# Key, value and weight loads of a one-token attention block: issued by GpSimd in place of SyncE

## Chip, core and metric

The kernel runs on one core of one Trainium2 chip. The metric is the device time of one execution in microseconds (us). Three runs of the kernel before are given; what is compared is their median. The trace comes from one further execution under the profiler.

## What is computed

One decoding step of a transformer block for a single token (width 640): layer norm, attention with 32 heads over a cache of 8192 keys and values of width 192, output projection, residual, layer norm, a gated ReLU network of width 1536, residual. All is float32.

```python
def _A_ref(x, k_cache, v_cache, wq, wo):
    q = (x @ wq).reshape(B, Sq, H, Dh).transpose(0, 2, 1, 3)
    scores = einsum("bhqd,bhkd->bhqk", q, k_cache) * (Dh ** -0.5)
    o = einsum("bhqk,bhkd->bhqd", softmax(scores), v_cache)
    return o.transpose(0, 2, 1, 3).reshape(B, Sq, H * Dh) @ wo
def _B_ref(x, W_gate, W_up, W_down):
    gate = x @ W_gate; up = x @ W_up
    return ((gate * (gate > 0)) * up) @ W_down
h  = x + _A_ref(_layernorm(x), k_cache, v_cache, wq, wo)
h2 = h + _B_ref(_layernorm(h), W_gate, W_up, W_down)
```

Keys and values are 2 x 32 x 8192 x 192 floats, 403 MB; the weights add the rest of some 446 MB. Each number of them is read once and used once, against a single query.

## The kernel before

The host packs everything into a few long arrays of 128 rows, in the order in which it is used: `row_p` (the first head's keys, query weights, the token), then ten turns of five pieces `row_1` to `row_5`, then the last head and the weights of the network (`row_t1` to `row_t3`, `row_up`, `row_gate`, `row_down`). A piece is at most 128 rows of 16320 floats, 65280 bytes a row. On the chip there are three buffers of that size, `slot_x`, `slot_y` and `slot_z` (X, Y, Z in the code), and each load fills one of them.

A turn (`turn`, ten of them) works through three heads: `pe_unit` on TensorE multiplies a head's keys by its query (L180) and, for the head before, its values by the softmax weights (L187); VectorE makes the next query and adds the output projection (`dve_unit`); ScalarE takes the exponentials. The loops of the engines run beside each other, tied by semaphores.

All 61 loads are issued by SyncE, in `sync_program`, through `load`. Three loads go out at once (`row_p` into Y, the first `row_1` into X, the first `row_2` into Z). From then on SyncE waits, before it refills a buffer, for a semaphore `free[..]` that says the buffer has been read to its end, and for `land[..]`, which the earlier load into it raised by 16; it takes the 16 off again in the same wait. The order is Y (`row_3`), X (`row_4`), Y (`row_5`), X (`row_1`), Z (`row_2`). After the last turn come ten loads of the tail, each with a semaphore of its own in `tl`, which TensorE waits for and takes down. At the end SyncE waits for `fout`, stores half of the result, and waits until both halves are stored (`out_s`, `out_a`; ScalarE stores the other half).

GpSimd has little to do: `pool_program` makes four constants (`ones`, `ident`, `pat`) and raises `cst_pe` and `cst_ve`, for which TensorE and VectorE wait before they start.

Of the kernel before, what the change touches and what calls it, by code (L numbers as in the profile page):

```python
# [8 lines left out]
ET = mybir.EngineType  # L9

P, D, H, S, DH, F = 128, 640, 32, 8192, 192, 1536
# [7 lines left out]
NTURN = (H - 2) // 3  # L19
SCALE = DH ** -0.5  # L20
EPS = 1e-5
DG, FG = D // 4, F // 4

W_P = 14272
# [61 lines left out]
def build(nc, arrays):  # L86
# [31 lines left out]
    o4 = sb("o4", [P, DG])  # L118
# [14 lines left out]
    def wait(eng, s, n, sub=0, **kw):  # L133
        w = eng.wait_ge(s, n)  # L134
        if sub:
            w.then_inc(s, -sub)
        return w
# [37 lines left out]
    te = nc.tensor  # L175
# [37 lines left out]
    def pe_unit(kblk, vblk, rows, freed=None, freed_at=None, q_next=True):  # L213
        def landed(n):
            if n in rows:
                s, sub = rows[n]
                wait(te, s, 16, sub)

        wait(te, a2p, 1, 1)
        landed("k0")  # L220
        pe_k(kblk, 0)
        wait(te, a2p, 1, 1)
        pe_o()
        wait(te, a2p, 1, 1)
        pe_l()
        landed("k1")
        pe_k(kblk, 1)
        landed("v0")
        at = None if freed is None else (freed_at, freed)
        pe_v(vblk, 0, 8, inc_at=at)  # L230
        landed("v8")
        pe_v(vblk, 8, 24, inc_at=at)
        if q_next:
            wait(te, d2p, 2, 2)
            if freed is not None and freed_at < 24 and freed is not fin:
                te.sem_inc(freed, 1)
            pe_q()
        else:
            wait(te, d2p, 1, 1)
        pe_t()  # L240
        landed("v24")
        pe_v(vblk, 24, 32, last=p2a)

    def tensor_program():
        wait(te, cst_pe, 1, 1)
        wait(te, pre, 1, 1)
        op(te.matmul(pl[:, 0:1], ones, vec["s1"], start=True, stop=True), inc=p2d)
        wait(te, pre, 1, 1)
        op(te.matmul(pl[:, 0:1], ones, vec["s2"], start=True, stop=True), inc=p2d)
        wait(te, d2p, 1, 1)  # L250
        pe_q()
        wait(te, a2p, 1, 1)
        wait(te, land[5], 16)
        pe_k(kp, 0)
        pe_k(kp, 1)
        wait(te, d2p, 2, 2)
        pe_q()
        pe_t()
        with te.Fori(0, NTURN):
            pe_unit(ka, va, {"k0": (land[1], 0), "v8": (land[2], 0)}, free[1], 7)  # L260
            pe_unit(kb, vb, {"k1": (land[3], 0), "v24": (land[4], 0)}, free[3], 23)
            pe_unit(kc, vcc, {"v0": (land[5], 0)})
        pe_unit(kt, vt, {"k0": (tl["t1"], 16), "v8": (tl["t2a"], 16)}, fin, 7, q_next=False)
        wait(te, a2p, 1, 1)
        pe_o()
        wait(te, a2p, 1, 1)
        pe_l()
        wait(te, tl["t2b"], 16, 16)
        pe_v(vz, 0, 16)
        wait(te, d2p, 3, 3)  # L270
        for g in range(4):
            te.matmul(acc[Q(g), 0:DG], ones[Q(g), 0:32], xd[Q(g)].rearrange("p c j -> p (c j)"),
                      start=True, stop=False, tile_position=(32 * g, 32 * g))
        for g in range(4):
            te.matmul(acc[Q(g), 0:DG], ones[:, 0:32], accs[:, g * DG:(g + 1) * DG], start=False, stop=False)
        for g in range(4):
            r = slice(0, 64) if g < 2 else slice(64, P)
            te.matmul(acc[Q(g), 0:DG], ones[r, 0:32], accs[r, D + (g % 2) * DG:D + (g % 2 + 1) * DG],
                      start=False, stop=False)
        wait(te, tl["t3"], 16, 16)  # L280
        pe_v(vz, 16, 32, last=p2a)
        wait(te, a2p, 1, 1)
        pe_o()
        wait(te, d2p, 1, 1)
        for g in range(4):
            te.matmul(acc[Q(g), 0:DG], oc[:, 0:1].to_broadcast([P, 32]), woz[:, g * DG:(g + 1) * DG],
                      start=False, stop=False)
        for g in range(4):
            r = slice(0, 64) if g < 2 else slice(64, P)
            m = te.matmul(acc[Q(g), 0:DG], oc[r, 1:2].to_broadcast([64, 32]),  # L290
                          woz[r, D + (g % 2) * DG:D + (g % 2 + 1) * DG], start=False, stop=True)
        m.then_inc(p2a, 1)
        wait(te, a2p, 1, 1)
        op(te.matmul(pt[:, 0:1], ones, vec["hs1"], start=True, stop=True), inc=p2d)
        wait(te, d2p, 1, 1)
        op(te.matmul(od[:, 0:1], ones, vec["hs2"], start=True, stop=True), inc=p2d)
        wait(te, tl["up"], 16, 16)
        for j in range(DJ):
            for g in range(4):
                m = te.matmul(sc[Q(g), 0:FG], hc[:, j, :], up[:, j, g * FG:(g + 1) * FG],  # L300
                              start=(j == 0), stop=(j == DJ - 1))
        op(m, inc=p2a)
        wait(te, tl["gate"], 16, 16)
        for j in range(DJ):
            for g in range(4):
                m = te.matmul(sc[Q(g), 512:512 + FG], hc[:, j, :], gate[:, j, g * FG:(g + 1) * FG],
                              start=(j == 0), stop=(j == DJ - 1))
        op(m, inc=p2d)
        wait(te, d2p, 1, 1)
        wait(te, tl["d0"], 16, 16)  # L310
        for j in range(FJ):
            if j == 6:
                wait(te, tl["d1"], 16, 16)
            if j == 10:
                wait(te, tl["d2"], 16, 16)
            if j < FJ - 1:
                for g in range(4):
                    te.matmul(q_ps[Q(g), 0:DG], guT[:, j, :], down[:, j * D + g * DG:j * D + (g + 1) * DG],  # L318
                              start=(j == 0), stop=False)
            else:  # L320
                for half in range(2):
                    if half:
                        wait(te, tl["d3"], 16, 16)
                    for g in range(2 * half, 2 * half + 2):
                        m = te.matmul(q_ps[Q(g), 0:DG], guT[:, j, :], down[:, j * D + g * DG:j * D + (g + 1) * DG],  # L325
                                      start=False, stop=True)
        op(m, inc=p2d)
# [199 lines left out]
        po_.sem_inc(cst_pe, 1)  # L527
        po_.sem_inc(cst_ve, 1)

    sp = nc.sync  # L530

    def load(t, src, s):
        sp.dma_start(t, src).then_inc(s, 16)

    def sync_program():
        load(Y[:, 0:W_P], dram["row_p"], land[5])
        r1, r2, r3, r4, r5 = (dram[f"row_{i}"] for i in range(1, 6))
        load(X[:, 0:W_1], r1[0], land[1])
        load(Z[:, 0:W_2], r2[0], land[2])

        def turn(i):
            wait(sp, free[5], 1, 1)
            wait(sp, land[5], 16, 16)
            load(Y[:, 0:W_3], r3[i], land[3])
            wait(sp, free[1], 2, 2)
            wait(sp, land[1], 16, 16)
            load(X[:, 0:W_4], r4[i], land[4])
            wait(sp, free[3], 2, 2)
            wait(sp, land[3], 16, 16)
            load(Y[:, 0:W_5], r5[i], land[5])  # L550
            wait(sp, free[2], 1, 1)
            wait(sp, land[2], 16, 16)
            wait(sp, free[4], 1, 1)
            wait(sp, land[4], 16, 16)

        with sp.Fori(0, NTURN - 1) as i:
            turn(i)
            load(X[:, 0:W_1], r1[i + 1], land[1])
            load(Z[:, 0:W_2], r2[i + 1], land[2])
        turn(NTURN - 1)  # L560
        load(X[:, 0:W_T1], dram["row_t1"], tl["t1"])
        load(Z[:, 0:W_T2A], dram["row_t2a"], tl["t2a"])
        load(Z[:, W_T2A:W_T2A + W_T2B], dram["row_t2b"], tl["t2b"])
        wait(sp, free[5], 1, 1)
        wait(sp, land[5], 16, 16)
        load(Y[:, 0:W_T3], dram["row_t3"], tl["t3"])
        load(Y[:, W_T3:W_T3 + W_UP], dram["row_up"], tl["up"])
        wait(sp, fin, 1, 1)
        load(X[:, 0:W_UP], dram["row_gate"], tl["gate"])
        for n, (a, b) in enumerate(DOWN):  # L570
            load(X[:, W_UP + a:W_UP + b], dram["row_down"][:, a:b], tl[f"d{n}"])
        wait(sp, fout, 1)
        load(out[0, 0, 0:D // 2].rearrange("(g n) -> g n", g=2), o4[31:33, :], out_s)
        wait(sp, out_s, 16, 16)
        wait(sp, out_a, 16, 16)
        wait(sp, fout, 1, 1)

    programs = ((ET.PE, tensor_program), (ET.DVE, vector_program), (ET.Activation, scalar_program),
                (ET.Pool, pool_program), (ET.SP, sync_program))
    for e, _ in programs:  # L580
        nc.br(f"prog_{e.name}", engines=[e])
    for e, f in programs:
# [12 lines left out]
```

## Time and profile before

| | us |
|---|---|
| median of 3 runs | 1039.3 |
| lowest and highest | 1038.07, 1039.48 |
| the profiled execution, its own time | 1039.63 |
| its span, from the first to the last instruction | 1038.3 |

1.33 us of the profiled execution's time lie outside its span. A share of busy time is an average over the span, and the DMA share is a mean over the core's 16 DMA engines. The releaser of a wait is inferred from semaphores. A transfer has two times in the trace: when its issue stands in the queue of the issuing engine, and when its landing lets a waiting engine go on. The windows view credits a packet to the stretch in which it falls only roughly, so that shares a little over 1.00 occur in short stretches.

### The profile page before, as it was taken

What the parts mean: (1) busy time and instruction counts of PE and PEld (TensorE: products, weight loads), DVE (VectorE), ACT (ScalarE), POOL (GpSimd) and SP (SyncE); (2) the same over time, 40 slices, a digit from 0 to 9 for tenths busy, and PEclk for the clock granted to TensorE, in tenths of its full rate; (3) what the DMA queues carried; (4) which work ended last, traced back from release to release, by engine and by line L of the source; (5) the groups of instructions that cost most, each with busy time, mean ns of one, the idle gap of its engine ahead of it and who ended that gap; (6) DMA issues with size and microseconds to landing.
All of it is one profiled execution on the core that took longest, in us unless ns stands there. A gap on an engine that the chain in (4) does not pass through costs nothing. (4 is left out here: it accounts for less than half of the span.)

```text
span 1038.3 us, 10306 instructions
## 1 busy us (share of the span) xinstructions
PE 547.4 (53%) x4492; PEld 176.3 (17%) x4492; DVE 188.2 (18%) x478; ACT 41.2 (4%) x137; POOL 1.2 (0%) x11
## 2 busy tenths in 40 slices
PE   0746446456363563654544546536465463564676
PEld 0211112112121120111111112112111121121123
DVE  1211221112122021221121220212221121220111
ACT  1000000000000000000000000000000000000010
POOL 0000000000000000000000000000000000000000
PEclk9876867768677677776787867867877778687787
DMA  9999999999999999999999999999999999999997
GB/s 402 441 432 425 434 435 431 445 420 435 435 439 433 425 438 436 440 427 432 435 435 426 433 438 431 444 426 433 433 438 438 420 438 436 438 432 425 432 427 326
DMA packets 8800, 446.07 MB, mean 430 GB/s; under 512 B 980, under 2 KB 1112, under 8 KB 1240
## 3 DMA queue, kind: packets, MB, share of 16 engines
q1 hardware_dynamic: 8788, 445.94, 99.4%
q8 instruction: 7, 0.11, 0.0%
q14 instruction: 1, 0.01, 0.0%
q10 hardware_dynamic: 4, 0.00, 0.0%
HBM read 445.94 MB, written 0.00 MB: 429 GB/s over the span
## 5 line engine op out<-in xcount | busy, mean ns | idle before, releaser
L180 PE MATMUL sc<-slot_x,qs 128*32 128x512 f32 x1008 | 150.9, 743 | 109.6 <-DMA slot_x<-row 99.9
L187 PE MATMUL po<-slot_y,p 128*2 128x384 f32 x1152 | 117.9, 562 | 80.2 <-DMA slot_y<-row 77.4
L187 PE MATMUL po<-slot_z,p 128*2 128x384 f32 x560 | 72.5, 671 | 91.7 <-DMA slot_z<-row 88.4
L180 PE MATMUL sc<-slot_y,qs 128*32 128x512 f32 x288 | 54.1, 913 | 83.0 <-DMA slot_y<-row 82.5
L187 PE MATMUL po<-slot_x,p 128*2 128x384 f32 x336 | 43.6, 651 | 86.1 <-DMA slot_x<-row 86.1
L373 DVE COPY oc<-od 128x2 f32<-128x2 f32 x32 | 5.1, 159 | 389.5 <-PE od L206 389.5
L385 DVE STREAM_TRANSPOSE st<-sc 128x512 f32<-128x512 f32 x64 | 45.7, 714 | 164.4 <-PE sc L180 164.4
L180 PEld LDWEIGHTS sc<-slot_x,qs 128*32 128x32 f32 x1008 | 35.4, 134 | 200.8 <-DMA slot_x<-row 106.3
L187 PEld LDWEIGHTS po<-slot_y,p 128*2 128x2 f32 x1152 | 29.1, 94 | 167.7 <-DMA slot_y<-row 86.5
L391 DVE TENSOR_REDUCE m<-pt 128x1 f32<-128x128 f32 x32 | 9.3, 292 | 162.6 <-PE pt L199 162.6
L187 PEld LDWEIGHTS po<-slot_z,p 128*2 128x2 f32 x560 | 15.0, 102 | 138.3 <-DMA slot_z<-row 95.6
L474 ACT COPY qs<-q_ps 128x96 f32<-128x96 f32 x32 | 7.7, 239 | 766.9 <-ACTq L134 766.9
L367 DVE SCALAR_TENSOR_TENSOR prod<-slot_y,xn,prod 128x192 f32<-128x192 f32 x88 | 36.9, 419 | 3.1
L180 PEld LDWEIGHTS sc<-slot_y,qs 128*32 128x32 f32 x288 | 11.4, 154 | 113.8 <-DMA slot_y<-row 83.4
L180 PE MATMUL sc<-slot_z,qs 128*32 128x512 f32 x240 | 27.6, 592 | 0.0
L187 PEld LDWEIGHTS po<-slot_x,p 128*2 128x2 f32 x336 | 8.6, 94 | 109.5 <-DMA slot_x<-row 88.0
L203 PEld LDWEIGHTS od<-mrl,ob 128*128 128x128 f32 x132 | 18.1, 199 | 34.2 <-issue 34.2
L478 ACT COPY ob<-po 128x384 f32<-128x384 f32 x32 | 15.3, 479 | 181.1 <-ACTq L134 181.1
L203 PE MATMUL od<-mrl,ob 128*128 128x1 f32 x132 | 20.8, 262 | 1.6 <-PEq L134 1.6
L194 PE MATMUL q_ps<-pat,prod 128*128 128x96 f32 x64 | 15.4, 323 | 8.5 <-PEq L134 8.5
L365 DVE TENSOR_SCALAR prod<-slot_y,xn 128x192 f32<-128x192 f32 x22 | 6.9, 315 | 65.4 <-DMA slot_y<-row 65.3
L376 DVE SCALAR_TENSOR_TENSOR accs<-slot_y,oc,accs 128x640 f32<-128x640 f32 x21 | 18.5, 879 | 0.0
(95 smaller groups left out, 248.6 us busy)
## 6 DMA issues: line engine op xcount, KB each, us to landing
slot_x<-row SPq DMA_DIRECT2D x10, 8160.0 KB, 26.9
slot_z<-row SPq DMA_DIRECT2D x10, 8160.0 KB, 45.8
slot_y<-row SPq DMA_DIRECT2D x10, 8160.0 KB, 24.7
slot_x<-row SPq DMA_DIRECT2D x10, 7680.0 KB, 35.6
slot_y<-row SPq DMA_DIRECT2D x10, 7584.0 KB, 27.1
slot_x<-row_t SPq DMA_DIRECT2D x1, 7680.0 KB, 25.2
slot_y<-row_p SPq DMA_DIRECT2D x1, 7136.0 KB, 19.6
slot_z<-row_t2a SPq DMA_DIRECT2D x1, 5088.0 KB, 36.9
```

The costliest lines, as they stand in the source:

```text
L180: m = te.matmul(sc[Q(g), half * 512:half * 512 + 512], qs[:, 32 * part:32 * part + 32], blk(half, part * 4 + g), start=(part == 0), stop=( ...
L187: m = te.matmul(po[32 * g:32 * g + 2, 0:PW], p[:, 2 * i:2 * i + 2], blk(i), start=(i < 4), stop=(i >= 28))
L194: te.matmul(q_ps[:, 0:96], prod[:, 0:P], pat[:, 0, :], start=True, stop=False)
L203: te.matmul(od[:, 0:1], ob[:, k * DH:k * DH + P], mrl[:, k:k + 1], start=(k == 0), stop=(k == 1))
L365: dv(ve.tensor_scalar(prod, w3[:, 0, :], xn[:, 0:1], None, op0=ALU.mult), w=first)
L367: dv(STT(prod, w3[:, j, :], xn[:, j:j + 1], prod, op0=ALU.mult, op1=ALU.add), w="self", inc=d2p if j == DJ - 1 else None)
L373: dv(ve.tensor_copy(oc, od[:, 0:2]), w=pd())
L376: dv(STT(accs[:, 0:D], w[:, 0:D], oc[:, 0:1], accs[:, 0:D], op0=ALU.mult, op1=ALU.add), w="self", inc=inc)
L385: return dv(ve.transpose(st[:, s], sc[:, s]), w=w)
L391: dv(ve.reduce_max(vec["m1"], pt[:, 0:P], axis=AX.X, negate=True), w=pd(), inc=d2a)
L474: op(ac.copy(qs, q_ps[:, 0:96]), inc=a2p)
L478: op(ac.copy(ob, po[:, 0:PW]), inc=a2p)
```

## The change

`load` calls GpSimd's `dma_start` instead of SyncE's. The loads, their rows, their order, their buffers and what they wait for stay as they are; they now stand in `load_program` on GpSimd, with the loop. `sync_program` keeps the store of half of the result alone. Four things go with it:

- The first three loads stand ahead of `pool_program`, so the constants are made after these three issues.
- A wait that took 16 off a load's semaphore becomes `settled`: a wait for 16, then an instruction of GpSimd's, `inc_swdge_sem`, that takes the 16 off.
- TensorE's waits on the ten semaphores of the tail no longer take them down. GpSimd does so at the end: after `fout` it runs `settled` for each of the ten, then raises `fin`.
- SyncE waits for `fin` as well before it ends.

```diff
-    def load(t, src, s):
-        sp.dma_start(t, src).then_inc(s, 16)
+    def load(t, src, s, **kw):
+        po_.dma_start(t, src, single_packet=SINGLE, **kw).then_inc(s, 16)
+
+    def settled(s):
+        wait(po_, s, 16)
+        po_.inc_swdge_sem([s], [16], mode="sub")
...
         load(Z[:, 0:W_2], r2[0], land[2])
+        pool_program()
...
-            wait(sp, free[5], 1, 1)
-            wait(sp, land[5], 16, 16)
+            wait(po_, free[5], 1, 1)
+            settled(land[5])
             load(Y[:, 0:W_3], r3[i], land[3])
...
-        with sp.Fori(0, NTURN - 1) as i:
+        with po_.Fori(0, NTURN - 1) as i:
...
+        wait(po_, fout, 1)
+        for s in tl.values():
+            settled(s)
+        po_.sem_inc(fin, 1)
...
         wait(sp, out_a, 16, 16)
+        wait(sp, fin, 1, 1)
```

`SINGLE` is False. TensorE's waits on `tl`, such as `wait(te, tl["up"], 16, 16)`, become `wait(te, tl["up"], 16)`.

GpSimd's queue at the start of the program, in the kernel before: five instructions of the preamble, a branch, and the constants (`ones`, `pat`, `ident`; `cst` is the semaphore between them).

```order
L581 UNCONDITIONAL_BRANCH [waits barrier_Pool_Activation_PE_DVE_SP_gather]
L519 MEMSET ones 128x128
L520 MEMSET pat 128x288
L522 ISA
L522 AFFINE_SELECT ident<-ones 128x128 [waits cst]
L525 MEMSET pat 128x16 x4
```

The same place in the changed kernel, on to the first refill of a buffer (the lines of the code are shifted).

```order
L594 UNCONDITIONAL_BRANCH [waits barrier_Pool_Activation_PE_DVE_SP_gather]
L532 DMA slot_y<-row_p 128x14272
L532 DMA slot_x<-row 128x16320
L532 DMA slot_z<-row 128x16320
L520 MEMSET ones 128x128
L521 MEMSET pat 128x288
L523 ISA
L523 AFFINE_SELECT ident<-ones 128x128 [waits cst]
L526 MEMSET pat 128x16 x4
L560 UNCONDITIONAL_BRANCH [waits cst]
L536 ISA [waits free5,land5]
```

Three DMA issues stand where `ones` was made, and the constants behind them; the instruction at L536, which takes 16 off a semaphore, is the first of the loop and holds the two waits of the first refill.

The end of SyncE's queue before: the last loads of the tail and the store of the result.

```order
L533 DMA slot_x<-row_gate 128x7680 [waits fin]
L533 DMA slot_x<-row_down 128x3840
L533 DMA slot_x<-row_down 128x2560
L533 DMA slot_x<-row_down 128x960
L533 DMA slot_x<-row_down 128x320
L533 DMA out<-o 2x160 [waits fout]
```

The end of GpSimd's queue now: the same loads, and behind them the ten instructions that wait for `fout` and take the semaphores of the tail down (seven of them are shown; three more, for `tl_d1` to `tl_d3`, follow).

```order
L532 DMA slot_x<-row_down 128x960
L532 DMA slot_x<-row_down 128x320
L536 ISA [waits tl_t1,fout]
L536 ISA [waits tl_t2a]
L536 ISA [waits tl_t2b]
L536 ISA [waits tl_t3]
L536 ISA [waits tl_up]
L536 ISA [waits tl_gate]
L536 ISA [waits tl_d0]
```

The store of half of the result stays on SyncE, alone there behind `fout`; the ten instructions run on GpSimd beside it.

## Rows read from the trace of the kernel before

**Rows 1.** The page: DMA share in 40 slices, packets, and the loads' queue.

```profile
DMA  9999999999999999999999999999999999999997
...
DMA packets 8800, 446.07 MB, mean 430 GB/s; under 512 B 980, under 2 KB 1112, under 8 KB 1240
...
q1 hardware_dynamic: 8788, 445.94, 99.4%
```

**Rows 2.** Windows: stretch, its length, five engines' busy us, PEclk, DMA share, GB/s.

```profile
1.90:1034.70 1032.80, 545.67 (x4448) 174.88 (x4452) 187.06 (x476) 41.24 (x137) 0.00 (x0) 0.77 1.00 432
1034.70:1038.30 3.60, 1.71 (x52) 1.39 (x43) 0.38 (x1) 0.00 (x0) 0.00 (x0) 1.00 0.00 1
...
1026.00:1031.20 5.20, 5.13 (x40) 2.03 (x40) 0.00 (x0) 0.00 (x0) 0.00 (x0) 0.67 0.97 409
...
1031.00:1032.00 1.00, 0.15 (x4) 0.00 (x0) 0.76 (x2) 0.00 (x0) 0.00 (x0) 1.00 0.90 357
```

**Rows 3.** Timeline of SyncE's queue: start us, us, issue of a load.

```profile
0.81 0.42 SPq L533 DMA_DIRECT2D slot_y<-row_p  x1
...
55.84 0.34 SPq L533 DMA_DIRECT2D slot_y<-row  x1
61.83 0.34 SPq L533 DMA_DIRECT2D slot_x<-row  x1
89.02 0.33 SPq L533 DMA_DIRECT2D slot_y<-row  x1
...
148.43 0.33 SPq L533 DMA_DIRECT2D slot_y<-row  x1
...
1036.88 0.34 SPq L533 DMA_DIRECT2D out<-o  x1
```

**Rows 4.** Timeline of TensorE: start us, us, what, and the wait that ended before it.

```profile
60.05 4.70 PE L187 MATMUL po<-slot_z,p 128*2 128x384 f32 x32 [7.69 <-DMA slot_z<-row]
...
79.61 5.19 PE L180 MATMUL sc<-slot_y,qs 128*32 128x512 f32 x24 [8.73 <-DMA slot_y<-row]
...
97.75 2.74 PE L187 MATMUL po<-slot_x,p 128*2 128x384 f32 x16 [8.13 <-DMA slot_x<-row]
...
154.22 5.30 PE L187 MATMUL po<-slot_z,p 128*2 128x384 f32 x32 [9.26 <-DMA slot_z<-row]
```

**Rows 5.** Timeline of TensorE in the tail: up, gate and down projection.

```profile
1017.28 6.32 PE L300 MATMUL sc<-slot_y,hc 128*32 128x384 f32 x40
1026.02 5.13 PE L306 MATMUL sc<-slot_x,hc 128*32 128x384 f32 x40 [2.42 <-PEq L134]
1032.94 3.20 PE L318 MATMUL q_ps<-slot_x,guT 128*32 128x160 f32 x88 [1.79 <-PEq L134]
1035.93 0.48 PE L325 MATMUL q_ps<-slot_x,guT 128*32 128x160 f32 x8
```

**Rows 6.** Timeline of GpSimd and VectorE at the start.

```profile
0.81 0.20 POOL L519 MEMSET ones<- 128x128 f32 x1 [0.29 <-POOLq L590]
0.95 0.34 POOL L520 MEMSET pat<- 128x288 f32 x1
...
1.54 0.86 DVE L424 MEMSET accs<- 128x960 f32 x1 [0.19 <-issue]
...
20.49 0.16 DVE L429 TENSOR_REDUCE s<-slot_y 128x1 f32<-128x5 f32 x1 [17.80 <-DMA slot_y<-row_p]
```

**Rows 7.** Instructions of two lines' queues: duration ns min/median/max, first and last start.

```profile
L590 POOLq EVENT_SEMAPHORE  x2: 17/17/17, 0.6 to 0.7; - x2
...
L590 POOLq INC_SWDGE_SEM  x1: 27/27/27, 0.2 to 0.2; - x1
...
L590 POOLq DRAIN  x1: 186/186/186, 0.4 to 0.4; - x1
```

**Rows 8.** The page's costliest groups: two of VectorE's.

```profile
L367 DVE SCALAR_TENSOR_TENSOR prod<-slot_y,xn,prod 128x192 f32<-128x192 f32 x88 | 36.9, 419 | 3.1
...
L365 DVE TENSOR_SCALAR prod<-slot_y,xn 128x192 f32<-128x192 f32 x22 | 6.9, 315 | 65.4 <-DMA slot_y<-row 65.3
```

More of the change, by code (lines that the diff above doesn't have):

```diff
@@ L21 @@
 EPS = 1e-5
+SINGLE = False
 DG, FG = D // 4, F // 4
@@ L262, in tensor_program @@
             pe_unit(kc, vcc, {"v0": (land[5], 0)})
-        pe_unit(kt, vt, {"k0": (tl["t1"], 16), "v8": (tl["t2a"], 16)}, fin, 7, q_next=False)
+        pe_unit(kt, vt, {"k0": (tl["t1"], 0), "v8": (tl["t2a"], 0)}, fin, 7, q_next=False)
         wait(te, a2p, 1, 1)
@@ L267, in tensor_program @@
         pe_l()
-        wait(te, tl["t2b"], 16, 16)
+        wait(te, tl["t2b"], 16)
         pe_v(vz, 0, 16)
@@ L279, in tensor_program @@
                       start=False, stop=False)
-        wait(te, tl["t3"], 16, 16)
+        wait(te, tl["t3"], 16)
         pe_v(vz, 16, 32, last=p2a)
@@ L296, in tensor_program @@
         op(te.matmul(od[:, 0:1], ones, vec["hs2"], start=True, stop=True), inc=p2d)
-        wait(te, tl["up"], 16, 16)
+        wait(te, tl["up"], 16)
         for j in range(DJ):
@@ L302, in tensor_program @@
         op(m, inc=p2a)
-        wait(te, tl["gate"], 16, 16)
+        wait(te, tl["gate"], 16)
         for j in range(DJ):
@@ L309, in tensor_program @@
         wait(te, d2p, 1, 1)
-        wait(te, tl["d0"], 16, 16)
+        wait(te, tl["d0"], 16)
         for j in range(FJ):
             if j == 6:
-                wait(te, tl["d1"], 16, 16)
+                wait(te, tl["d1"], 16)
             if j == 10:
-                wait(te, tl["d2"], 16, 16)
+                wait(te, tl["d2"], 16)
             if j < FJ - 1:
@@ L322, in tensor_program @@
                     if half:
-                        wait(te, tl["d3"], 16, 16)
+                        wait(te, tl["d3"], 16)
                     for g in range(2 * half, 2 * half + 2):
@@ L528, in pool_program, with load_program @@
         po_.sem_inc(cst_ve, 1)
-    sp = nc.sync
-    def load(t, src, s):
-        sp.dma_start(t, src).then_inc(s, 16)
-    def sync_program():
+    def load(t, src, s, **kw):
[3 more added lines that the diff above has]
+        po_.inc_swdge_sem([s], [16], mode="sub")
+    def load_program():
+        r1, r2, r3, r4, r5 = (dram[f"row_{i}"] for i in range(1, 6))
         load(Y[:, 0:W_P], dram["row_p"], land[5])
-        r1, r2, r3, r4, r5 = (dram[f"row_{i}"] for i in range(1, 6))
         load(X[:, 0:W_1], r1[0], land[1])
         load(Z[:, 0:W_2], r2[0], land[2])
+        pool_program()
         def turn(i):
-            wait(sp, free[5], 1, 1)
-            wait(sp, land[5], 16, 16)
+            wait(po_, free[5], 1, 1)
+            settled(land[5])
             load(Y[:, 0:W_3], r3[i], land[3])
-            wait(sp, free[1], 2, 2)
-            wait(sp, land[1], 16, 16)
+            wait(po_, free[1], 2, 2)
+            settled(land[1])
             load(X[:, 0:W_4], r4[i], land[4])
-            wait(sp, free[3], 2, 2)
-            wait(sp, land[3], 16, 16)
+            wait(po_, free[3], 2, 2)
+            settled(land[3])
             load(Y[:, 0:W_5], r5[i], land[5])
[L551 to L554, printed above, removed]
-        with sp.Fori(0, NTURN - 1) as i:
+            wait(po_, free[2], 1, 1)
+            settled(land[2])
+            wait(po_, free[4], 1, 1)
+            settled(land[4])
+        with po_.Fori(0, NTURN - 1) as i:
             turn(i)
@@ L563, in sync_program @@
         load(Z[:, W_T2A:W_T2A + W_T2B], dram["row_t2b"], tl["t2b"])
-        wait(sp, free[5], 1, 1)
-        wait(sp, land[5], 16, 16)
+        wait(po_, free[5], 1, 1)
+        settled(land[5])
         load(Y[:, 0:W_T3], dram["row_t3"], tl["t3"])
         load(Y[:, W_T3:W_T3 + W_UP], dram["row_up"], tl["up"])
-        wait(sp, fin, 1, 1)
+        wait(po_, fin, 1, 1)
         load(X[:, 0:W_UP], dram["row_gate"], tl["gate"])
@@ L571, in sync_program @@
             load(X[:, W_UP + a:W_UP + b], dram["row_down"][:, a:b], tl[f"d{n}"])
+        wait(po_, fout, 1)
+        for s in tl.values():
+            settled(s)
+        po_.sem_inc(fin, 1)
+    sp = nc.sync
+    def sync_program():
         wait(sp, fout, 1)
-        load(out[0, 0, 0:D // 2].rearrange("(g n) -> g n", g=2), o4[31:33, :], out_s)
+        sp.dma_start(out[0, 0, 0:D // 2].rearrange("(g n) -> g n", g=2), o4[31:33, :]).then_inc(out_s, 16)
         wait(sp, out_s, 16, 16)
         wait(sp, out_a, 16, 16)
+        wait(sp, fin, 1, 1)
         wait(sp, fout, 1, 1)
     programs = ((ET.PE, tensor_program), (ET.DVE, vector_program), (ET.Activation, scalar_program),
-                (ET.Pool, pool_program), (ET.SP, sync_program))
+                (ET.Pool, load_program), (ET.SP, sync_program))
     for e, _ in programs:
```

## Prediction, made before the changed kernel ran

> **What bounds the kernel now.** I read the page first, for its DMA line: 9 in 39 of 40 slices, and one queue, SyncE's, holds 99.4% of the 16 engines' span [rows 1]. So the transfers are the bound, and the question is what happens to them. Then the windows: from 1.90 to 1034.70 us the DMA share is 1.00 at 432 GB/s, and behind that it is 0.00 [rows 2]. The span falls into three pieces: 1.9 us of start, a stream of 1032.8 us, and 3.6 us of end. TensorE's waits say the same: it sits idle 8 or 9 us ahead of a piece and is let go by its landing [rows 4], while TensorE is busy 546 of the 1033 us.
>
> In the end piece the last multiplication runs from 1032.94 and ends at about 1036.4 [rows 5], the result is stored from 1036.88 [rows 3], and the span ends 1.42 us later. The gate projection starts at 1026.02, behind a wait for its weights [rows 5], so the end too hangs on the stream: a stream that is later by some time ends the kernel later by that time.
>
> **The stream itself.** The queue holds 8788 packets: 61 loads of 128 rows and 16 packets under 512 B are 8784, and four belong to the store [rows 1]. A row of up to 65280 bytes therefore goes as one packet. Rows, order and buffers don't change, so if a row stays one packet and the next load stands in the queue before the last has drained, the stream keeps its 1032.8 us. I take 0. Below nothing there is little: 99.4% of 1038.3 us leaves 6.2 us of idle engines, of which start and end have 5.5, so closing every gap gives 0.7 us. Above nothing the bound is far. The last small loads show what short rows cost: 357 GB/s at a share of 0.90, or 397 GB/s of a full share, against 432 [rows 2].
>
> **Where the cover of an issue is.** SyncE issues in 0.33 to 0.42 us [rows 3]. What GpSimd needs, with software that writes the descriptors, the trace does not show. What hides it is the data still queued when the issue is made, read as the landing of the load ahead less the issue. The refill of Y is issued at 55.84 and the Z load ahead of it lands at 60.05, which leaves 4.2 us, and 5.8 us one turn later (148.43 against 154.22). X at 61.83 has until 79.61, 17.8 us; Y at 89.02 until 97.75, 8.7 us [rows 3, 4]. Z follows X at once and is covered by the whole of X. So the smallest cover is 4.2 us.
>
> Against it stands, on GpSimd's queue, a wait (17 ns), the subtraction (27 ns by the one instruction of that kind in the trace, which there resets rather than subtracts) and the issue [rows 7]. For the issue I bound: below, SyncE's 0.42 us or even none; above, 144 packets written one by one at the price of the cheapest instruction of GpSimd's queue, 17 ns each [rows 7], an estimate of 2.4 us. Both are under 4.2 us. Queued behind a waiting GpSimd stand only later loads, as on SyncE before; nobody else waits for GpSimd in the loop. Sum over the loop: 0. If that cover were gone, each load would pay the excess, 50 times in the turns.
>
> The Trainium skill speaks against this change: "SBUF — State Buffer", section "Who interferes with whom", has the rule that a VectorE instruction that uses both ports locks GpSimd out, so that it can't write descriptors and the DMA engines sit idle. The trace bears out that VectorE has such an instruction: the same 192 columns take 315 ns at L365 and 419 ns at L367 [rows 8]. By that rule an issue in a turn waits some 0.3 us more, which stays inside the 4.2 us; only the first load has no cover, and a clearing of `accs`, 0.86 us from 1.54 us on, lies beside it [rows 6]: by the rule the sum below would be up to 0.9 us higher, 1041.4 us.
>
> **The start.** Nothing covers the first issue. SyncE starts it at 0.81 us [rows 3], and GpSimd is ready at the same 0.81 us, when it made `ones` [rows 6]. Of the 1.9 us at the start [rows 2], 0.42 us behind that are SyncE's issue and some 0.65 us the way to the first data; the change replaces the first and perhaps lengthens the second. With the bounds above, 0 to 2.4 us in place of 0.42, the change is -0.4 to +2.0 us. For the middle I use GpSimd's own writing: 288 columns take 0.34 us and 128 take 0.20 us [rows 6], 0.86 ns a word; if each of 144 packets takes eight words, which is an assumption, they are 1152 words, 1.0 us, and with 0.1 us ahead of them 1.1 us, an estimate. That is 0.7 us over SyncE's, and I add 0.3 us for a first call of that software. I take +1.0 us.
>
> The Trainium skill, "DMA: Bandwidth & Descriptors", section "Latency and other measured facts", gives about 1 us to the first byte by software and about 0.6 us by hardware. No row here shows the software's. By these two the start would lose 0.4 us, and the sum would be 1039.9 us.
>
> The constants move behind three issues, at most 3 x 2.4 us. They were done at 1.85 us and are first needed by the work at 20.49 us, when `row_p` lands [rows 6]. Cover 18.6 us; cost 0.
>
> **The end.** The ten subtractions and the rise of `fin` run on GpSimd from `fout` on, beside the store, and SyncE's last wait needs both. Ten waits and subtractions at 17 + 27 ns are 0.44 us [rows 7], inside the 1.42 us of the store: cost 0. They come into the open when one takes over 0.14 us. If each also waited as long as a drain, 0.19 us [rows 7], ten would be 2.3 us, 0.9 us past the store. I take +0.2 us, nearer to the row of the same name. TensorE's waits without a subtraction cost nothing that the trace shows.
>
> **Sum.** +1.0 at the start, 0 in the stream, +0.2 at the end: 1039.63 + 1.2 = 1040.8 us for the profiled execution. That one lies 0.33 us above the median of the runs, so I forecast 1040.5 us, 0.12% more. About 0.2%, 2.1 us, is what a measurement of this kernel can tell from no change. One thing can move the end by itself: TensorE's granted clock is 0.67 of full during the gate projection, between its levels of 1.2 and 2.4 GHz [rows 2]. The up projection with the same 40 products took 6.32 us where the gate took 5.13 [rows 5], so a shifted start can cost 1.2 us there; and the last load's landing lets it gain at most 0.9 us.
>
> **Rivals.**
> - *The stream loses a little at each load* (slower). Software may write the small packets at a load's end, or the hand-over to the next load, so that an engine pauses. For it: the stream is the bound everywhere and has no slack, so it decides from 0.9 us over 61 loads, 15 ns each. Against it: the same rows on the same engines. At 0.08 us a load it is 5 us, 1045.5 us; at an issue's length, 0.33 us, 20 us, 1060 us. The Trainium skill, "DMA: Bandwidth & Descriptors", section "Latency and other measured facts", says that two of the 16 engines are usually slower, with software rings in the scratch memory as its guess of a cause; no row here tells engines apart, and a load lands with its slowest. Chance 0.16.
> - *GpSimd is slow at both open places* (slower): the first call takes its bound or more, +2.0 us or over, and a real subtraction takes 0.2 to 0.5 us, so that ten end 0.6 to 3.6 us behind the store. For it: neither is shown in the trace, and a subtraction that walks a list is more than a reset. Against it: the rows of 17 and 27 ns. 1042 to 1045 us. Chance 0.16.
> - *An issue holds GpSimd until its load has landed, or rows are cut small* (much slower). Held issues would delay the constants from 1.85 us to past 60 us, where TensorE could start at 20.5: some 40 us, and no overlap of loads after that. Short rows as in the last loads: 1032.8 x 432/397, 91 us more, 1131 us. Against it: nothing in the change asks for either. Chance 0.04.
> - *Faster.* Gaps closed (0.7), an issue that costs nothing (0.4) and the end's 0.9 make 2.0 us, not quite enough; it needs packets that move more than 432 GB/s, by 0.3% for instance if software joins rows in one packet: 1037 us. Chance 0.04.
>
> **How the numbers follow.** The forecast, within 2.1 us of the median, has 0.60; slower cases 0.16 + 0.16 + 0.04 = 0.36; faster 0.04. The range begins at 1038.0 us, the sum with a free issue (1039.1) less the end's 0.9, rounded down; it goes up to 1046 us, which takes in GpSimd's slow places and half of the first rival. Left out are the other half (0.08), the much slower case (0.04) and the faster one (0.04).
>
> **What would show it.** Right: the queue of GpSimd's loads at 99% of the span with 8784 packets of the same sizes; DMA share 1.00 at 432 GB/s in the long window, which begins at about 2.9 us; the smallest cover still over 2 us; the ten subtractions done before the store is. Wrong: packets of another number or size, a stretch between two loads without data, a window shorter or longer than 1032.8 us by over 1 us, or a span that ends with GpSimd's queue.

## Result, and the profile of the changed kernel

The changed kernel takes 1042.35 us (median of 9 runs, 1040.66 to 1043.89) against 1038.44 us for the kernel before (9 runs, 1037.88 to 1039.76): a ratio of 1.0033 with a 95% interval of 1.0024 to 1.0042, 3.9 us slower. The forecast was 1040.5 us, 0.12% slower and within what counts as no change. The time lies in the stated range, but it moved by more than the 2.1 us to which the forecast gave 0.60: it is one of the slower cases, which had 0.36. The profiled execution took 1041.99 us with a span of 1040.3 us, 2.0 us over the span of before.

The page of the changed kernel first (its span, packets and the queue of GpSimd's loads), which answers to [rows 1]:

```profile
span 1040.3 us, 10308 instructions
...
DMA packets 8641, 446.08 MB, mean 429 GB/s; under 512 B 980, under 2 KB 984, under 8 KB 1080
...
q0 software_dynamic: 8624, 445.94, 99.3%
```

The transfers are still the bound. Then the windows (stretch, its length, busy us of five engines, PEclk, DMA share, GB/s), cut where the first data start and the last end, as [rows 2] were:

```profile
1.46:2.83 1.37, 0.00 (x0) 0.00 (x0) 0.87 (x3) 0.00 (x0) 1.37 (x3) 1.00 0.14 42
2.83:1036.30 1033.47, 547.75 (x4456) 173.65 (x4460) 186.60 (x474) 41.26 (x137) 32.03 (x66) 0.76 1.00 432
1036.30:1040.30 4.00, 1.46 (x44) 1.14 (x36) 0.38 (x1) 0.00 (x0) 0.00 (x0) 1.00 0.00 1
```

Start 2.8 us for 1.9 before, stream 1033.5 for 1032.8, end 4.0 for 3.6: in this execution each of the three pieces grew. GpSimd's timeline shows the start and the first refill (start us, us, issue, and what ended the idle time before it), beside [rows 3]:

```profile
1.46 0.67 POOL L532 DMA_DIRECT2D slot_y<-row_p  x1 [0.82 <-POOLq L603]
2.12 0.54 POOL L532 DMA_DIRECT2D slot_x<-row  x1
2.65 0.53 POOL L532 DMA_DIRECT2D slot_z<-row  x1
...
57.45 0.58 POOL L532 DMA_DIRECT2D slot_y<-row  x1 [53.23 <-DMA slot_y<-row_p]
```

An issue takes 0.53 us, the first 0.67. The first one starts at 1.46 us, 0.65 us later than SyncE's did. TensorE's timeline at the same place shows when the Z load and the refill of Y landed, beside [rows 4]:

```profile
61.08 4.64 PE L188 MATMUL po<-slot_z,p 128*2 128x384 f32 x32 [7.78 <-DMA slot_z<-row]
81.15 4.86 PE L181 MATMUL sc<-slot_y,qs 128*32 128x512 f32 x24 [9.31 <-DMA slot_y<-row]
```

From landing to landing it is 20.07 us; before it was 79.61 - 60.05 = 19.56. The cover of this refill, by the prediction's measure, was 61.08 - 57.45 = 3.6 us where it had been 4.2.

### The profile page after: what moved, and what is told of

The parts are those of the page before. It is cut to its first block, busy times and chain, and to the rows that moved or that the text cites. A ratio compares the mean times of both kernels' runs of the same rounds, so it can differ in the third digit from the quotient of the medians.

```text
span 1040.3 us, 10308 instructions
## 1 busy us (share of the span) xinstructions
PE 549.2 (53%) x4492; PEld 174.8 (17%) x4492; DVE 188.2 (18%) x478; ACT 41.3 (4%) x137; POOL 33.6 (3%) x72
## 3 DMA queue, kind: packets, MB, share of 16 engines
q0 software_dynamic: 8624, 445.94, 99.3%
## 5 line engine op out<-in xcount | busy, mean ns | idle before, releaser
L181 PE MATMUL sc<-slot_x,qs 128*32 128x512 f32 x1008 | 147.1, 727 | 104.4 <-DMA slot_x<-row 94.1
L188 PE MATMUL po<-slot_y,p 128*2 128x384 f32 x1152 | 124.7, 588 | 84.3 <-DMA slot_y<-row 81.2
L188 PE MATMUL po<-slot_z,p 128*2 128x384 f32 x560 | 69.9, 651 | 93.3 <-DMA slot_z<-row 91.0
L181 PE MATMUL sc<-slot_y,qs 128*32 128x512 f32 x288 | 57.8, 968 | 86.2 <-DMA slot_y<-row 85.7
L532 POOL DMA_DIRECT2D slot_y<-row x20 | 10.7, 533 | 672.8 <-DMA slot_y<-row 354.4
```

What stands on the lines that cost most here:

```text
L181: m = te.matmul(sc[Q(g), half * 512:half * 512 + 512], qs[:, 32 * part:32 * part + 32], blk(half, part * 4 + g), start=(part == 0), stop=( ...
L188: m = te.matmul(po[32 * g:32 * g + 2, 0:PW], p[:, 2 * i:2 * i + 2], blk(i), start=(i < 4), stop=(i >= 28))
L532: po_.dma_start(t, src, single_packet=SINGLE, **kw).then_inc(s, 16)
```

## Experiments: the stream

Two theories stood. **Ends**: the loss lies at the two open ends of the program, and the stream is as before. **Stream**: loads issued in software lose time in the stream; in a later form (**cover**), they lose it at the one refill whose issue finds the least data queued, that of Y at the start of a turn.

**The changed kernel again** (e1), unaltered.

> The changed kernel once more, as the mark for the others on this chip. Ends theory (the loss lies at the two open ends of the program, start +1.0 and end +0.6 us in the trace, with 0.35 us outside the span, and the stream is as before): the single runs differ by what the end of the program makes of them, and the middle of the span is 1032.8 to 1033.5 us again. Stream theory (each load issued by GpSimd loses a little): the stream is longer than before's by 2 us in a middling run. Both: 2.5 to 5 us over before.

1042.29 us (8 runs, 1040.65 to 1043.97) against 1038.48 for before on the same chip. The runs spread over 3.3 us, and the profiled one was among the longer ones, with a span of 1041.3 us. Its landings tell more than the first trace did:

```profile
61.02 4.27 PE L188 MATMUL po<-slot_z,p 128*2 128x384 f32 x32 [8.34 <-DMA slot_z<-row]
82.30 5.35 PE L181 MATMUL sc<-slot_y,qs 128*32 128x512 f32 x24 [10.89 <-DMA slot_y<-row]
```

21.28 us for the refill, 1.7 us more than before, in one place; its issue was at 56.83 us, 4.2 us ahead of Z's landing, which is no less than in the trace of the kernel before. The stream loses, and not evenly, and the cover by this measure doesn't say alone how much.

**GpSimd for the turns alone** (e2): SyncE issues the first three loads and the ten of the tail.

```diff
+    def taken(s):              # first turn: the loads were SyncE's
+        wait(po_, s, 16, 16)
+    turn(0, taken, taken, taken)
...
-        load(X[:, 0:W_T1], dram["row_t1"], tl["t1"])
+        po_.sem_inc(go, 1)     # SyncE waits for go and issues the tail
```

> GpSimd issues only the loads of the ten turns; the first three loads and the ten of the tail are SyncE's again, and TensorE takes the tail's semaphores down as before. Nothing of GpSimd's then stands at an open end. Ends theory: within 0.5 us of before. Stream theory: 2 us or more over before, since 48 of the 61 loads are still issued in software.

1041.33 us (12 runs, 1038.57 to 1043.00), ratio 1.0026 (1.0017 to 1.0035). The ends theory wanted within 0.5 us of before; it is 2.9 us over. Most of the loss is in the stream. The single runs reach from hardly any loss to 4.5 us of it, so it differs from run to run. The profiled run is the fastest of the twelve (1038.57 us), so its trace can't show where the others lost.

**An earlier release of Y** (e5): in the first unit of a turn VectorE adds the output projection, which reads Y, ahead of the next query's product.

```diff
-            if w_next is not None:
+            if w_next is not None and not wo_first:
                 dve_d1(w_next)
             dve_wo(w_out)
             if freed_wo is not None:
                 wait(ve, ds, cnt.n).then_inc(freed_wo, 1)
+            if w_next is not None and wo_first:
+                dve_d1(w_next)
```

> The changed kernel, but in the first unit of a turn VectorE adds the output projection (which reads Y) before it makes the next query, so that the refill of Y is released some 2.1 us earlier and its issue finds 2.1 us more of queued data. Cover theory (the stream loses where a software-issued refill finds the first engines nearly drained, which is this refill): the lag of the last engine no longer jumps there, and the median falls by 1.5 to 2.5 us, to 1040 or 1041 us. Place theory (packets are slow at this hand-over whatever the cover, for where the rows lie): no change, 1042.3.

1040.21 us (11 runs, 1039.72 to 1040.79), ratio 1.0014 (1.0005 to 1.0023): 2.1 us less than e1, and the spread falls from 3.3 to 1.1 us. The trace shows the refill's issue and the two landings:

```profile
54.45 0.57 POOL L534 DMA_DIRECT2D slot_y<-row  x1 [50.24 <-DMA slot_y<-row_p]
```

```profile
61.00 4.07 PE L188 MATMUL po<-slot_z,p 128*2 128x384 f32 x32 [8.66 <-DMA slot_z<-row]
80.31 4.67 PE L181 MATMUL sc<-slot_y,qs 128*32 128x512 f32 x24 [9.12 <-DMA slot_y<-row]
```

The cover is 6.55 us and the refill takes 19.31 us. That is what it takes when nothing is lost, and 19.56 of the kernel before already held 0.25 us of loss. The stream as a whole took 1031.9 us:

```profile
2.83:1034.70 1031.87, 544.95 (x4454) 174.69 (x4458) 187.41 (x474) 41.17 (x137) 31.88 (x66) 0.75 1.00 432
```

The cover theory holds; the other one, that this hand-over is slow whatever its cover, falls.

**The same release in the kernel before** (e6), the same edit.

> The kernel before with the same earlier release of Y. Cover theory: its 4.2 us of cover were enough for SyncE, so the median moves by 0.5 us at most, towards the lowest runs (1037.9). Place theory: no change. If the earlier release harms something else on VectorE, it shows here as a loss.

1038.18 us (11 runs, 1037.86 to 1038.79) against 1038.64 (1038.01 to 1040.43), ratio 0.9995 (0.9986 to 1.0004). A gain is not shown, but the runs above 1039 are gone, and nothing else on VectorE was harmed.

**Less cover at another refill** (e7): GpSimd clears a spare tile twelve times ahead of the second refill of a turn (X, `row_4`).

```diff
             settled(land[1])
+            for _ in range(12):
+                op(po_.memset(idle, 0.0), inc=hold)
+                wait(po_, hold, 1, 1)
             load(X[:, 0:W_4], r4[i], land[4])
```

> The changed kernel, but GpSimd clears a spare tile twelve times, some 12.5 us, before it issues the second refill of a turn (X, row_4), which had 15 us until the first engine drains; some 2 us are left, as at the refill of Y. Cover theory: that hand-over now loses too, slow first packets or idle engines there in most turns, 1.5 to 3 us over the changed kernel. Place theory: nothing there, within 0.5 us of the changed kernel.

1054.82 us (4 runs, 1051.69 to 1056.20), ratio 1.0145 (1.0129 to 1.0160): 12.5 us over the changed kernel, four times the upper end of what was expected. GpSimd's timeline shows one reason that may have made the guess low, a delay of 13.8 us rather than 12.5:

```profile
159.38 0.95 POOL L554 MEMSET idle<- 128x1024 f32 x1 [6.45 <-DMA slot_x<-row]
...
173.23 0.53 POOL L534 DMA_DIRECT2D slot_x<-row  x1 [0.74 <-POOLq L137]
```

And the landings of Y and X in that kernel's first turn:

```profile
81.19 4.37 PE L183 MATMUL sc<-slot_y,qs 128*32 128x512 f32 x24 [9.88 <-DMA slot_y<-row]
...
100.25 2.74 PE L190 MATMUL po<-slot_x,p 128*2 128x384 f32 x16 [9.86 <-DMA slot_x<-row]
```

19.06 us, where the kernel before took 97.75 - 79.61 = 18.14 [rows 4]. A refill that lost nothing with its 17 to 18 us of cover loses 0.9 us with 4.6 (its issue was at 76.64 us). So do eight of the nine X refills that follow it in this trace, by 0.2 to 1.8 us each. The place is not what matters.

**Less cover for SyncE** (e11): the kernel before, its first refill of a turn behind one clearing of a spare tile on GpSimd.

```diff
+        with po_.Fori(0, NTURN):
+            wait(po_, free[5], 1, 1)
+            op(po_.memset(idle, 0.0), inc=hold)
+            wait(po_, hold, 1, 1)
+            po_.sem_inc(go, 1)
...
-            wait(sp, free[5], 1, 1)
+            wait(sp, go, 1, 1)
```

> The kernel before, SyncE issuing all, but the first refill of a turn (Y) waits some 1.2 us more, for one clearing of a spare tile on GpSimd. Its first engine then drains 0.7 to 2.2 us behind the issue. Cover theory in its general form (any issue needs it, GpSimd's only needs more): 2 to 4 us over before, with the lag jumping at that hand-over. If only software-issued loads lose there: within 0.5 us of before.

1041.11 us (11 runs, 1038.86 to 1045.99), ratio 1.0022 (1.0012 to 1.0031). SyncE's timeline and the landings:

```profile
56.05 0.34 SPq L540 DMA_DIRECT2D slot_y<-row  x1
...
624.36 0.33 SPq L540 DMA_DIRECT2D slot_y<-row  x1
```

```profile
60.02 5.22 PE L189 MATMUL po<-slot_z,p 128*2 128x384 f32 x32 [8.69 <-DMA slot_z<-row]
81.38 4.81 PE L182 MATMUL sc<-slot_y,qs 128*32 128x512 f32 x24 [10.01 <-DMA slot_y<-row]
...
628.27 4.41 PE L189 MATMUL po<-slot_z,p 128*2 128x384 f32 x32 [8.61 <-DMA slot_z<-row]
...
649.02 4.30 PE L182 MATMUL sc<-slot_y,qs 128*32 128x512 f32 x24 [10.22 <-DMA slot_y<-row]
```

The profiled run is the slowest of the eleven (1045.99 us). In the first turn the refill takes 21.36 us, 2 us more than without loss, though the issue came only 0.2 us later than in the trace of before and its cover is 4.0 us for 4.2. The later turns say more: in the seventh the cover is 3.9 us, where the trace of before has 5.0, and the refill takes 20.75 us where it took 19.3 there. Seven of the ten turns lose 0.4 to 2.1 us each, in before's trace only the first does. The loss at this refill is not GpSimd's own. SyncE pays it as well when it comes late. GpSimd comes later than SyncE did: in the changed kernel's first trace the nine later turns have 0.3 to 0.4 us less cover than before, and lose nothing there.

**One packet for a load and engine** (e12): `SINGLE = True`, and nothing else.

> The changed kernel with SINGLE set, which asks for one packet per load and engine. If the hand-over loses for lack of cover, the packets' form changes nothing: 1042.3 us. If the loss lies in how software's packets start, it changes by over 1 us either way.

1042.67 us (6 runs, 1039.92 to 1044.92), ratio 1.0041 (1.0026 to 1.0055); its trace has the same 8624 packets. The setting changes nothing that can be measured, and it doesn't mend the hand-over.

**A second place in the stream.** The traces lose time where the turns end as well. From the landing of the last turn's `row_4` in X to that of `row_t1` (two loads, each with 6.5 us of cover or more in these traces), TensorE's starts lie 36.2 us apart in the kernel before and 37.2 us in e1 (the row of before for `row_t1` names no DMA, but is the same product).

```profile
942.78 2.74 PE L187 MATMUL po<-slot_x,p 128*2 128x384 f32 x16 [9.09 <-DMA slot_x<-row]
...
978.94 4.38 PE L180 MATMUL sc<-slot_x,qs 128*32 128x512 f32 x24 [9.65 <-PEq L134]
```

```profile
945.83 2.74 PE L188 MATMUL po<-slot_x,p 128*2 128x384 f32 x16 [8.87 <-DMA slot_x<-row]
...
983.06 2.78 PE L181 MATMUL sc<-slot_x,qs 128*32 128x512 f32 x12 [10.34 <-DMA slot_x<-row_t]
```

By the landings it is 36.1 us in all four traces in which SyncE issues every load (before, e4, e6, e11), and 36.7, 37.2 and 37.6 us in the three of the changed kernel's form (the first, e1, e12); in e5 it is 36.4 us, in e8 36.6. So of what e1's trace lies above e5's, 2.0 us in the first turn and 0.3 us in the second are at the refill of Y and 0.8 us here, and e12's loses 0.2 us there and 1.5 us here. SyncE's traces don't lose at this place; the one of before loses 1.1 us at `row_gate` instead. No experiment was made on this, and its cause is open.

## Experiments: the two ends

**Both ends mended** (e3): SyncE issues the first three loads, and seven of the ten subtractions run before the last result.

```diff
-        load(Y[:, 0:W_P], dram["row_p"], land[5])
-        load(X[:, 0:W_1], r1[0], land[1])
-        load(Z[:, 0:W_2], r2[0], land[2])
         pool_program()
...
+        wait(po_, used, 1, 1)      # TensorE has passed the wait for d0
+        for n in ("t1", "t2a", "t2b", "t3", "up", "gate", "d0"):
+            settled(tl[n])
         wait(po_, fout, 1)
-        for s in tl.values():
-            settled(s)
+        for n in ("d1", "d2", "d3"):
+            settled(tl[n])
```

> The changed kernel with both ends mended: SyncE issues the first three loads, and GpSimd takes seven of the ten semaphores of the tail down as soon as TensorE has gone past their waits, so that three are left behind the last result. The tail's loads stay GpSimd's. Ends theory: 1.6 us less than the changed kernel, 1.9 at most, and within 1 us of before in the span. Stream theory: also 1.6 us less than the changed kernel, but still 2 us over before.

1040.54 us (12 runs, 1038.23 to 1043.30), ratio 1.0022 (1.0011 to 1.0032): 1.75 us less than e1, though the two intervals overlap, with a spread that is as wide as the changed kernel's or wider. As both theories expected, and 2.1 us over before, as only the stream theory did.

**A late start without GpSimd's DMA** (e4): SyncE's first load waits until GpSimd has made the constants.

```diff
+        wait(sp, go, 1, 1)
         load(Y[:, 0:W_P], dram["row_p"], land[5])
```

> The kernel before, SyncE issuing everything, but its first load waits until GpSimd has made the constants, some 1.1 us later (1.9 us in place of 0.8). It prices a late first load without GpSimd's DMA. Ends theory: 1.1 us over before, one for one. Rival: the time moves by more (up to 2.5 us) or less, because a shifted stream meets another granted clock in the last products.

1039.66 us (12 runs), ratio 1.0012 (1.0004 to 1.0021), 1.2 us over before; the trace has the first issue at 2.07 us for 0.81 [rows 3], 1.3 us later. Here a late first load costs one for one, and TensorE's clock in the tail adds nothing that shows.

**Start and end apart** (e9, e10), on top of the earlier release of Y, since that removed the spread; the edits are the two halves of e3's.

> The changed kernel with the earlier release of Y (e5, 1040.2 us) and its start mended: SyncE issues the first three loads, the ten subtractions stay at the end. Ends theory: 1.0 us less than e5, 1039.2. If the end weighs more than the start: 1039.7 or more.

> The changed kernel with the earlier release of Y (e5, 1040.2 us) and its end mended: seven of the ten subtractions done before the last result; GpSimd still issues the first three loads. Ends theory: 0.6 us less than e5, 1039.6. With e9 the two should sum to the 1.7 us by which e8 lies below e5.

1039.14 us (11 runs, 1038.87 to 1040.18) with the start mended, 1039.31 (11 runs, 1038.69 to 1040.13) with the end: 1.07 and 0.90 us less than e5. Together that is 1.97 us, where e8 below finds 1.74 for both; the end was expected at 0.6. SyncE's waits at the end show the second (waited for: us in total, times, longest), of the changed kernel and of e10:

```profile
SPq L135 <- SPq L135: 1.7, 3, 0.8
```

```profile
SPq L136 <- SPq L136: 1.0, 2, 0.8
```

The third wait, for GpSimd's `fin`, and 0.7 us go. The ten subtractions of the changed kernel, alone in the window behind 1030 us:

```profile
L536 POOLq INC_SWDGE_SEM  x10: 155/155/163, 1038.2 to 1040.1; - x10
```

0.155 us each and 0.2 us from one to the next, 2.0 us together, behind a store that needs 1.4. Some 0.35 us more are outside the span: with the ten at the end most runs have 1.65 to 1.75 us there, before's mostly 1.3. In e10 six of the eleven runs have 1.2 to 1.3 us there, and five 1.7 or a little more.

**Everything mended** (e8): e3's edits and the earlier release of Y.

> Ends mended as in e3 and the earlier release of Y of e5 together. Cover theory: within 0.7 us of before. Place theory: 2 us over before, as e3.

1038.47 us (11 runs, 1037.85 to 1038.89), ratio 0.9999 (0.9990 to 1.0008). With GpSimd still issuing 58 of the 61 loads the whole loss is gone. So it is accounted for: 2.1 us by the earlier release (e1 to e5) and 1.7 us by the ends (e5 to e8), 3.8 us of the 3.8 by which e1 lies above before. How the 2.1 us divide between the refill of Y and the end of the turns, the medians don't tell.

## Why the prediction was right or wrong

- **What bounds the kernel**, and that the end follows the stream: right. The page still has one queue at 99.3%, and e4 shows a shift of 1.3 us come out as 1.2.
- **The start, +1.0 us**: right in sum, by luck. The first data came at 2.83 us for 1.9, and mending it gave 1.07 us. Its parts were not as worked out. The issue takes 0.67 us, not 1.1; but GpSimd's first issue starts at 1.46 us, where the prediction had put 0.81 from the place of `ones`. The 0.65 us of the late begin make most of the change. From the beginning of the issue to the first data the traces have 1.37 us here and 1.04 before, 0.33 us more. The Trainium skill ("DMA: Bandwidth & Descriptors", "Latency and other measured facts") gives about 1 us to the first byte by software and about 0.6 us by hardware, 0.4 us apart; the difference agrees.
- **The end, +0.2 us**: the mechanism was right and the size was not. Over 0.14 us each, the text said, the subtractions come into the open; they take 0.155 us and 0.2 us in a row, since a real subtraction costs six times the reset from which the 27 ns came [rows 7]. Measured: 0.9 us. That is the upper bound that the text gave, but only 0.7 us of it are the subtractions behind the store; the rest lies outside the span, for which the text had no term.
- **The stream, 0**: this is the step that failed, "both are under 4.2 us", and it cost 2.1 us. The issue itself lay well inside the bounds (0.53 us between 0 and 2.4). The cover was read wrongly: a landing is that of the last of 16 engines, and the cost side held only the issue and not the way to the first data. The packet records of the trace, which no view prints, have the end marks of each load: the first engine is through with Z some 1.8 us before the last. Of 3.6 us that leaves about 1.8 us, against the 1.37 us that an issue needs to its first data. The sign that the text had named, a stretch without data, is there: in the first trace 8 to 10 of the 16 engines have no packet from 59.1 to 59.3 us, in e1 seven from 59.1 to 59.8 us, in e11 five to seven from 58.1 to 59.4 us; in before's trace it is one at most. e5, e7 and e11 moved the cover, and the loss at the refill moved with it. Where the edge lies is not shown: e1 and e11 lose 2 us with 2.3 us left to the first engine's mark, more than the 1.37 and 1.04 us to their first data, so the first drain alone doesn't give it.
- **The rivals**: the first one, a stream that loses at hand-overs, with 0.16, came true in kind; but it put the loss on all 61 loads and on software's packets. Within the turns it sits mainly on one refill, and SyncE's loads have it there as well (e11); at the end of the turns there is a second place, which shows only in traces with GpSimd's loads, and not in all of them. The second, GpSimd slow at both ends, came true for 0.7 us of the end. The two add, and the text had priced them singly. The faster and the much slower cases did not come.
- **The constants**, at no cost: right. They were done at 4.2 us and needed behind 20.
- **VectorE's lock**: not tested in the turns. Of the 51 issues between the first refill and 960 us, 50 took 0.53 or 0.54 us and one 0.58, but none of them ran beside the instruction of 315 ns; where VectorE was busy at all, it was with a reduction. The 315 and 419 ns that the text compared are of two different operations, and don't show a port. The first issue did run beside the clearing of `accs`, and took 0.67 us, 0.14 us more than the others and not 0.9.

What stays open is why a hand-over with little cover loses nothing in one run and 2 us in another. In the packet records the first packets of the refill take up to 3.8 us there instead of 2.41, and the engines without a packet add up to 6 us of engine time in the first trace, 9 in e1 and 10 in e11, which is 0.4 to 0.6 us for each of 16 engines: by these sums the slow packets make the larger part of the loss in e1 and e11. No run tells what makes them slow. One rival can be left out as the cause by itself: in every trace a packet of 8 KB of the queue that the page calls instruction falls near this hand-over of the first turn (58 to 61 us). But e5 and e6 have it too and lose nothing, and e7 and e11 lose in later turns, which have none.

## What to carry to other kernels

In this kernel, which is bound by transfers, a slower issuer took over the loads of the loop at no cost that shows, once every issue had its cover (e8). Look for the one refill with the least. Count more than the issue, and more than its way to the first data: measured up to the landing of the load ahead, 6.5 us and more lost nothing at this refill in any turn (e5, e6, e10), while 3.6 to 5.7 us lost from nothing to 2.1 us. At the end of the turns as much cover as that was not always enough. Moving one step of VectorE by 2 us gave back what the choice of the issuer in the loop had cost. What an issuer does ahead of the first transfer or behind the last result was paid in full here; bookkeeping such as taking semaphores down belongs in the middle.

## What the runs showed that was not expected

- Software joins short rows: the page has 8624 packets where hardware made 8788 (of which four are the store's), and those under 8 KB fell from 1240 to 1080. The rows of 3840 and 1280 bytes were 256 packets and are 96. The prediction had named packets of another number as a sign of being wrong; the long stretch still moves 432 GB/s.
- Near its edge the cover decides the spread of a kernel more than its best time: lowest runs are 1038.57 us in e2 and 1037.89 in before, and the spreads 4.4 and 3.4 us; with the earlier release they are 1.1 us (e5) and 0.9 us (e6).
- The kernel before stood at that edge itself, with 4.2 us of cover at its first turn and single runs up to 1041.3 us.
